# Retention and soft mixture of experts on one core: tiles of 128 positions of one batch in place of 64 positions of two

## The chip, the cores and the metric

The kernel runs on one core of a Trainium2 chip. The time is device microseconds for one execution, the median of several runs. One more execution was recorded by the hardware profiler; all rows of the profile come from it. The engines are called as in the profile: PE (TensorE, matmuls; PEld its weight loads), DVE (VectorE), ACT (ScalarE), POOL (GpSimd), SP (SyncE, which issues most transfers).

## The reference

```python
# q, k, v: 8 batches x 8 heads x 576 positions x 64, float32
scores = q @ k^T / sqrt(64)
gamma  = 1 - 2 ** (-5 - head)
ret    = scores * where(i >= j, gamma ** (i - j), 0)
x      = (ret @ v), heads side by side: 4608 tokens x 512
# soft mixture of experts, 8 experts of 4 slots, hidden size 1024
logits = x @ phi                                  # 4608 x 32
d      = softmax(logits over the 4608 tokens)
slot_input = d^T @ x                              # 32 x 512
slot_out   = relu(slot_input[e] @ w1[e]) @ w2[e]  # per expert
c      = softmax(logits over the 32 slots)
out    = c @ slot_out
```

The decay factors into a factor of the key's position and one of the query's, so a chunk of positions needs the masked scores inside the chunk and, for all earlier chunks, one 64 x 64 state per head, which is the sum of k^T v so far.

## The kernel before, in words

The program has two parts. A loop over `NT` = 36 tiles computes the retention, the transposed output, the logits and the running sums of the softmax over tokens. Behind the loop come the experts' two layers and the output product.

A tile before holds 64 positions of two batches: rows 0 to 63 of the 128 partitions are one batch, rows 64 to 127 the other. There are 9 chunks of 64 for each of the four pairs of batches. Eight heads stand as four pairs `a` with `j` = 0, 1. Each step of a tile is a method:

- `stage_k(t)`: four PE transposes of k (L151), copied to `kt` by ACT (L152). It is done for the tile ahead.
- `scale(t)`: POOL multiplies v by its decay (L136) and builds `gb`, the query's decay for this chunk (L138). Also one tile ahead.
- `stage_a(t)`: scores, 16 products of 64 x 64 (L160), masked into `s` by one DVE operation (L163).
- `stage_c(t)`: adds k^T v to the state in PSUM (L194, 16 products), and ACT copies the state to `sb` (L197).
- `stage_i(t, same)`: queries times the state so far (L177), in two pieces of 8 products, the second behind a small DVE copy `seen` (L181) that reads what the first wrote.
- `stage_b(t)`: adds v^T s to the same PSUM tile `px` (L207, 16 products); DVE multiplies by `gb` into the output tile `x` (L214).
- `stage_d(t)`: transposes x back to rows (L221, ACT L223).
- Group work, one part per tile and one group per four tiles: `group_1` the logits (L235) and running maximum, `group_e` the exponentials, `group_2` a transpose (L273), `group_3` the product with x (L282) added to `acc` (L288), `softmax_c` the softmax over slots (L294 to L308).

Products with 64 rows and 64 columns use one quarter of the PE array each, at a position given by the rows of their operands and of their output.

The order of all engines is written out by hand: each engine does its instructions in the order of the source. For a tile it is a, c, first i, k of the next tile, group parts and d, second i, b. SP issues the loads in that order too: `tok` holds k, v and the transposed q of each tile; k and v go to one of four slots `kv` (K behind c, V behind b, four tiles ahead), q to one of three slots `qs`, and the experts' weights, 41 units of 512 KB, to `ws`, spread over the loop.

PSUM has eight banks: two for `ps_n` (k, d, logits, group product), two for the state, two for scores (with a corner `pse` for small transposes), two for `px`.

Of the kernel before, what the change touches and what calls it, by code (L numbers as in the profile page):

```python
# [20 lines left out]
C = 64  # L21
NC = S // C
NT = B // 2 * NC
# [4 lines left out]
NR = 7  # L28
CST = ((0, C), (C, NC * H), (C + NC * H, NC * NP), (C + NC * (H + NP), NP * C))
NCST = C + NC * (H + NP) + NP * C  # L30
# [4 lines left out]

@with_exitstack
def retention_softmoe(ctx, tc, tok, phi, wun, cst, msel, out):
    nc = tc.nc
    PS = bass.MemoryType.PSUM
# [11 lines left out]
    ps_st = ctx.enter_context(tc.tile_pool(name="ps_st", bufs=1, space=PS))  # L51
    tiles_only = ExitStack()
# [6 lines left out]
    s = slots.tile([P, 2, NP, C], F32, name="sT")  # L59
# [3 lines left out]
    tri, vt, cf, g0 = (cs_[:, o:o + n] for o, n in CST)  # L63
    vt = vt.rearrange("p (n h) -> p n h", n=NC)
    cf = cf.rearrange("p (n a) -> p n a", n=NC)
    g0 = g0.rearrange("p (a i) -> p a i", a=NP)
    gb = [cpool.tile([P, NP, C], F32, name=f"gb{i}") for i in range(2)]
    phs = cpool.tile([P, NP, NS], F32, name="phs")
    ms = cpool.tile([P, 2 * P], F32, name="ms")
    ident = cpool.tile([P, P], F32, name="ident")  # L70
    sb = [cpool.tile([P, 2, NP, D], F32, name=f"sb{i}") for i in range(2)]
# [26 lines left out]
    nc.scalar.dma_start(out=cs_, in_=cst)  # L98
    K, V = slice(0, 512), slice(512, 1024)
# [7 lines left out]
    late = [(phs, phi), (ms, msel)]  # L107
# [8 lines left out]
    pss = ps_s.tile([P, 2, 512], F32, name="pss")  # L116
    pse = pss[:, 0, NP * C:NP * C + P]
# [15 lines left out]

    def scale(t):
        v = vn(t)
        nc.gpsimd.tensor_tensor(  # L136
            out=v, in0=v, in1=vt[:, t % NC, :].unsqueeze(2).broadcast_to([P, H, D]), op=ALU.mult)
        nc.gpsimd.tensor_tensor(  # L138
            out=gb[t % 2], in0=g0, in1=cf[:, t % NC, :].unsqueeze(2).broadcast_to([P, NP, C]), op=ALU.mult)

    def bank_n():
        return ps_n.tile([P, NP, P], F32, name="pn")

    def mtile():
        return bank_n().rearrange("p a i -> p (a i)")
# [8 lines left out]
    def stage_a(t):  # L154
        q = qT(t)
        ps = pss[:, :, 0:NP * C].rearrange("p j (a i) -> p j a i", a=NP)
        for a in range(NP):
            for j in range(2):
                for r in range(2):
                    nc.tensor.matmul(ps[half(r), j, a, :], lhsT=kt[half(j), a, half(r)],  # L160
                                     rhs=q[half(j), a, half(r)], start=True, stop=True,
                                     skip_group_check=True)
        nc.vector.tensor_tensor(out=s, in0=ps, in1=tri.unsqueeze(1).unsqueeze(2).broadcast_to([P, 2, NP, C]),  # L163
                                op=ALU.mult)

    def stage_i(t, same):
        if not same:
            PX[t] = ps_x.tile([P, 2, 512], F32, name="px")[:, :, 0:NP * C].rearrange(
                "p r (c i) -> p r c i", c=NP)
        if t % NC == 0:  # L170
            return
        px = PX[t]
        for z in range(2):
            for al in range(2):
                for j in range(2):
                    r, a = (j if same else 1 - j), 2 * z + al
                    nc.tensor.matmul(px[half(al), r, 2 * j + z, :], lhsT=sb[t % 2][half(j), r, a, :],  # L177
                                     rhs=qT(t)[half(j), a, half(r)], start=(not same and z == 0),
                                     stop=False, skip_group_check=True)
        if not same:  # L180
            nc.vector.tensor_copy(out=sm("seen")[D:P], in_=px[D:P, 0, NP - 1, 0:1])  # L181

    def stage_c(t):
        n = t % NC
        if n == NC - 1:
            return
        if n == 0:
            ST[0] = ps_st.tile([P, 2, 512], F32, name="pst")[:, :, 0:NP * D].rearrange(
                "p r (a d) -> p r a d", a=NP)
        k, v = kn(t), vn(t)  # L190
        for a in range(NP):
            for r in range(2):
                for j in range(2):
                    nc.tensor.matmul(ST[0][half(j), r, a, :], lhsT=k[half(r), 2 * a + j, :],  # L194
                                     rhs=v[half(r), 2 * a + j, :], start=(n == 0 and a == 0),
                                     stop=(n == NC - 2), skip_group_check=True)
        nc.scalar.copy(out=sb[(t + 1) % 2], in_=ST[0])  # L197

    def stage_b(t):
        v = vn(t)  # L200
        px = PX.pop(t)
        for z in range(2):
            for j in range(2):
                for al in range(2):
                    for r in range(2):
                        a = 2 * z + al
                        nc.tensor.matmul(px[half(al), r, 2 * j + z, :], lhsT=v[half(r), 2 * a + j, :],  # L207
                                         rhs=s[half(r), j, a, :], start=(t % NC == 0 and z == 0 and j == 0),
                                         stop=True, skip_group_check=True)
        x = ring.tile([P, NP, P], F32, name="x")  # L210
        xv = x.rearrange("p c (r i) -> p r c i", r=2)
        for c in ((slice(0, 2), slice(2, 4)) if t == NT - 1 else (slice(0, 4),)):
            n = c.stop - c.start
            nc.vector.tensor_tensor(out=xv[:, :, c], in0=px[:, :, c],  # L214
                                    in1=gb[t % 2][:, c].unsqueeze(1).broadcast_to([P, 2, n, C]), op=ALU.mult)
        xT[t] = x
# [54 lines left out]
    def group_2(g):  # L271
        et, alpha = gstate[g]
        nc.tensor.transpose(pse, et, ident)  # L273
        en = gpool.tile([P, P], F32, name="en")
        nc.scalar.copy(out=en, in_=pse)
        gstate[g] = (en, alpha)
# [14 lines left out]
    def softmax_c(g, pn=None):  # L291
        if pn is None:
            pn = pse
            nc.tensor.transpose(pn, ltg[g], ident)  # L294
# [16 lines left out]
    delta = ms[:, 0:P]  # L311
    negmask = ms[:, P:2 * P]

    scale(0)
    stage_k(0)
    for t in range(NT):
        g, r = divmod(t - 4, 4)
        group = t >= 4
        stage_a(t)
        stage_c(t)  # L320
        stage_i(t, False)
        load_kv(t + NKV, K)
        while issued[0] < min(NW, NW * (t + 1) // (NT - 3)):
            load_w(ws[issued[0]])
# [11 lines left out]
        if group and r == 2:  # L336
            stage_d(4 * g + 3)
        if t == NT - 2:
            group_3(g)
        if group and r == 3:  # L340
            if t < NT - 1:
                group_3(g)
                softmax_c(g)
            else:
                stage_d(NT - 4, True)
                mo = mrun[(NG - 2) % 2]
                nc.tensor.transpose(pse, mo.broadcast_to([P, P]), ident)
                mm = gpool.tile([P, 4, NS], F32, name="et")
                mom = mm[:, 0, :]
                nc.vector.tensor_reduce(out=mom, in_=pse.rearrange("p (i s) -> p s i", i=4),  # L350
                                        axis=AX.X, op=ALU.max)
# [9 lines left out]
    stb = ps_st.tile([P, 2, 512], F32, name="pst")  # L361
    wb, pm = stb[:, 0], stb[:, 1]
    pl = logits(pm, NG - 1, 0, 3)
    hm = [slots.tile([P, 1024], F32, name="kv3").rearrange("p (c e s) -> p c e s", c=4, e=NE)]
    sim = [slots.tile([P, 2, NE, NS], F32, name=x) for x in ("qs0", "sT")]
    nc.gpsimd.memset(sim[0], 0.0)
    nc.gpsimd.memset(sim[1], 0.0)
# [62 lines left out]
    for i in range(4):  # L430
        nc.tensor.matmul(pr[i * NS:(i + 1) * NS, 0:1], lhsT=en[:, i * NS:(i + 1) * NS],
                         rhs=tri[:, C - 1:C], start=True, stop=True, skip_group_check=True)
# [40 lines left out]
    identr = cpool.tile([P, 2, P], F32R, name="gb0")[:, 0]  # L473
    nc.gpsimd.tensor_copy(out=identr, in_=ident)
    cs = []
    ctw = [cpool.tile([P, NP, P], F32R, name=n) for n in ("sb0", "sb1")]
# [43 lines left out]
    p1 = [wb, mtile()]  # L520
# [136 lines left out]
def unpack(o):  # L657
    o = o.reshape(2, NG, 2, C, 4, 256).transpose(1, 4, 2, 3, 0, 5)
    o = o.reshape(B // 2, NC, 2, C, DM).transpose(0, 2, 1, 3, 4)
    return o.reshape(B * S, DM)  # L660
# [55 lines left out]
```

## Time and profile before

| what | value |
|---|---|
| median of 3 runs | 259.07 us (258.59 to 259.28) |
| the profiled execution | 260.98 us |
| its span, first to last instruction | 259.2 us |
| PE busy | 206.6 us (80%), 5571 matmuls and 5571 weight loads |
| DVE, ACT, POOL busy | 101.0, 90.5, 62.1 us |
| moved by DMA | 72.52 MB, 280 GB/s on the mean |
| mean granted PE clock | 0.950 |

How to read it: the profile lists one record for each matmul and one for each weight load, and an fp32 product makes two of each (an fp32 transpose one). A record's length is its latency; products on different parts of the array overlap, so the distance between starts tells what a product costs. "issue" is time in which an engine waited for nothing that the profile shows. The queue "q8 instruction" carries the engines' programs.

### The profile page before, as it was taken

How to read it: one execution, taken by the hardware profiler on the slowest of the kernel's cores; microseconds unless marked ns; L12 is line 12 of the kernel's file. 1: busy time of each engine (PE TensorE's matmuls, PEld its weight loads, DVE VectorE, ACT ScalarE, POOL GpSimd, SP SyncE). 2: the span in 40 equal slices, each digit the busy share in tenths (PEclk: the TensorE clock that was granted, in tenths of full speed). 3: DMA queues.
4: the chain of work that ended last, by engine and by line, in shares of the span. 5: the costliest groups of instructions: out<-in, count | busy, mean ns of one | idle time of the engine just before them, and what ended most of it. 6: DMA issues, size and time to landing. Idle time of an engine off the chain costs nothing.

```text
span 259.2 us, 12312 instructions
## 1 busy us (share of the span) xinstructions
PE 206.6 (80%) x5571; PEld 152.9 (59%) x5571; DVE 101.0 (39%) x250; ACT 90.5 (35%) x198; POOL 62.1 (24%) x83
## 2 busy tenths in 40 slices
PE   7759698788759886977887879887997799999830
PEld 6648485575648565666565567566673235666620
DVE  0324043543524534352354354352354423155740
ACT  2312243343333353245143335334221033243730
POOL 1824043242223234033223423322120010000000
PEclk9998799999998999799999999998999999999985
DMA  6998788988796989788876998884220999976895
GB/s 199 389 388 276 282 265 279 325 290 293 236 325 190 304 310 304 227 303 286 287 265 226 320 317 303 292 310 147 85 83 3 326 414 409 408 293 262 338 402 235
DMA packets 27556, 72.52 MB, mean 280 GB/s; under 512 B 3056, under 2 KB 3440, under 8 KB 27504
## 3 DMA queue, kind: packets, MB, share of 16 engines
q1 hardware_dynamic: 27360, 71.51, 78.2%
q8 instruction: 44, 0.72, 1.1%
q10 hardware_dynamic: 144, 0.22, 0.2%
q14 instruction: 8, 0.07, 0.1%
HBM read 62.28 MB, written 9.44 MB: 277 GB/s over the span
## 4 chain that ended last, share of the span: by engine, by line
PE 66%; issue 12%; DVE 9%; ACT 6%; DMA 2%; POOL 0%; DVEq 0%; SPq 0%; ACTq 0%; POOLq 0%
PE px L177 9%; PE pn L151 8%; PE pn L221 6%; PE pst L574 6%; PE px L207 5%; PE pst L194 5%; PE pss L160 5%; PE pn L282 4%; DVE x L214 4%; PE pn L235 3%; PE po L599 3%; PE pst L526 3%; PE pn L526 3%; ACT kt L152 2%; DMA kv<-in_tok 2%
## 5 line engine op out<-in xcount | busy, mean ns | idle before, releaser
L138 POOL TENSOR_TENSOR gb<-cst 128x256 f32<-128x256 f32 x36 | 22.1, 615 | 117.0 <-DVE x L214 117.0
L177 PE MATMUL px<-qs,sb 64*64 64x64 f32 x1024 | 32.6, 236 | 17.4 <-issue 8.9
L214 DVE TENSOR_TENSOR x<-px,gb 128x512 f32<-128x512 f32 (+1 forms) x37 | 24.9, 676 | 50.1 <-PE px L207 49.8
L136 POOL TENSOR_TENSOR kv<-kv,cst 128x512 f32<-128x512 f32 x36 | 37.6, 1044 | 7.4 <-DMA kv<-in_tok 7.4
L177 PEld LDWEIGHTS px<-qs,sb 64*64 64x64 f32 x1024 | 23.6, 140 | 26.5 <-issue 14.4
L197 ACT COPY sb<-pst 128x512 f32<-128x512 f32 x32 | 18.8, 587 | 57.4 <-PE pst L194 57.4
L152 ACT COPY kt<-pn 128x512 f32<-128x512 f32 x36 | 21.1, 586 | 35.1 <-PE pn L151 34.9
L160 PE MATMUL pss<-qs,kt 64*64 64x64 f32 x1152 | 27.1, 225 | 6.3 <-issue 5.4
L207 PE MATMUL px<-sT,kv 64*64 64x64 f32 x1152 | 26.6, 228 | 2.9 <-issue 2.9
L163 DVE TENSOR_TENSOR sT<-pss,cst 128x512 f32<-128x512 f32 x36 | 24.6, 684 | 10.4 <-PE pss L160 8.9
L194 PE MATMUL pst<-kv 64*64 64x64 f32 x1024 | 24.0, 224 | 5.4 <-issue 5.1
L160 PEld LDWEIGHTS pss<-qs,kt 64*64 64x64 f32 x1152 | 22.8, 139 | 8.2 <-issue 6.9
L151 PE MATMUL pn<-ident,kv 128*128 128x128 f32 x144 | 24.2, 290 | 2.7 <-issue 2.7
L207 PEld LDWEIGHTS px<-sT,kv 64*64 64x64 f32 x1152 | 22.8, 144 | 4.0 <-issue 3.9
L194 PEld LDWEIGHTS pst<-kv 64*64 64x64 f32 x1024 | 20.5, 138 | 6.2 <-issue 5.8
L221 PE MATMUL pn<-ident,x 128*128 128x128 f32 x132 | 22.8, 299 | 1.1 <-issue 0.4
L223 ACT COPY x<-pn 128x512 f32<-128x512 f32 x33 | 19.4, 588 | 8.8 <-PE pn L221 8.3
L221 PEld LDWEIGHTS pn<-ident,x 128*128 128x128 f32 x132 | 16.0, 149 | 4.8 <-ACT kt L152 3.7
L151 PEld LDWEIGHTS pn<-ident,kv 128*128 128x128 f32 x144 | 15.4, 143 | 2.5 <-DMA kv<-in_tok 0.2
L561 DVE COPY ws<-po 128x512 f32<-128x512 f32 x15 | 10.1, 690 | 8.4 <-PE po L599 8.3
L559 ACT COPY ws<-po 128x512 f32<-128x512 f32 x15 | 8.7, 589 | 10.5 <-PE po L599 10.4
L282 PE MATMUL pn<-x,en 128*32 128x512 f32 x64 | 10.7, 649 | 1.1 <-ACT kt L152 0.6
(143 smaller groups left out, 203.1 us busy)
## 6 DMA issues: line engine op xcount, KB each, us to landing
ws<-in_w SPq DMA_DIRECT2D x61, 512.0 KB, 6.0
kv<-in_tok SPq DMA_DIRECT2D x66, 256.0 KB, 4.2
qs<-in_tok SPq DMA_DIRECT2D x36, 256.0 KB, 4.2
out<-ws SPq DMA_DIRECT2D x14, 512.0 KB, 3.9
kv<-in_tok SPq DMA_DIRECT2D x3, 512.0 KB, 7.0
kv<-in_w SPq DMA_DIRECT2D x3, 512.0 KB, 5.0
out<-kv SPq DMA_DIRECT2D x3, 512.0 KB, 6.2
out<-ws SPq DMA_DIRECT2D x2, 256.0 KB, 3.2
```

The source lines that it names most:

```text
L136: nc.gpsimd.tensor_tensor(out=v, in0=v, in1=vt[:, t % NC, :].unsqueeze(2).broadcast_to([P, H, D]), op=ALU.mult)
L138: nc.gpsimd.tensor_tensor(out=gb[t % 2], in0=g0, in1=cf[:, t % NC, :].unsqueeze(2).broadcast_to([P, NP, C]), op=ALU.mult)
L151: nc.tensor.transpose(pk[:, a, :], k[:, 2 * a:2 * a + 2, :].rearrange("p j d -> p (j d)"), ident)
L152: nc.scalar.copy(out=kt, in_=pk)
L160: nc.tensor.matmul(ps[half(r), j, a, :], lhsT=kt[half(j), a, half(r)], rhs=q[half(j), a, half(r)], start=True, stop=True, skip_group_check ...
L163: nc.vector.tensor_tensor(out=s, in0=ps, in1=tri.unsqueeze(1).unsqueeze(2).broadcast_to([P, 2, NP, C]), op=ALU.mult)
L177: nc.tensor.matmul(px[half(al), r, 2 * j + z, :], lhsT=sb[t % 2][half(j), r, a, :], rhs=qT(t)[half(j), a, half(r)], start=(not same and z ...
L194: nc.tensor.matmul(ST[0][half(j), r, a, :], lhsT=k[half(r), 2 * a + j, :], rhs=v[half(r), 2 * a + j, :], start=(n == 0 and a == 0), stop=( ...
L207: nc.tensor.matmul(px[half(al), r, 2 * j + z, :], lhsT=v[half(r), 2 * a + j, :], rhs=s[half(r), j, a, :], start=(t % NC == 0 and z == 0 an ...
L214: nc.vector.tensor_tensor(out=xv[:, :, c], in0=px[:, :, c], in1=gb[t % 2][:, c].unsqueeze(1).broadcast_to([P, 2, n, C]), op=ALU.mult)
L221: nc.tensor.transpose(pn[:, a, :], xT[t][:, a, :], ident)
L282: nc.tensor.matmul(pp[i * NS:(i + 1) * NS, :], lhsT=en[:, i * NS:(i + 1) * NS], rhs=xN[4 * g + i].rearrange("p a i -> p (a i)"), start=Tru ...
```

## The change

A tile now holds 128 positions of one batch. A batch has four chunks of 128 positions and 64 left over; the left-over halves of two batches share a ninth tile (chunk number `NCH` = 4), so there are again 36 tiles. Tiles of the two batches of a pair take turns (`tile_order`).

- Scores: 16 products again. A 128 x 128 block of scores is cut in four 64 x 64 squares, of which the upper one is zero and is never computed. So half of the products stream 128 query columns and half 64. `s` is twice as wide, its zero square is written once ahead of the loop. The order of k and v rows is swapped by halves for four of the heads.
- The mask takes three DVE operations: two of 64 rows x 256, one of 128 x 512.
- `stage_i` is one piece of 8 products with 128 columns streaming; the `seen` copy is gone. It uses one state per batch (`sb[b % 2]`), in the ninth tile both.
- `stage_c` has 8 products over all 128 rows, 64 columns wide; the state copy is half as large.
- `stage_b` has 8 products over all 128 rows of v, with 128 columns streaming.
- `gb` is twice as wide and built once for the two batches of a pair.
- The order becomes a, d (remainders 1 and 2), k, group parts, i, group parts, c, b. `group_3` moves from remainder 3 to remainder 2, between i and c. K and V are loaded together behind b. A PSUM bank of its own (`ps_m`) takes logits, group product and small transposes.
- Constants: the table `g0` is 128 wide and has a transfer of its own; `ms` is loaded late, into a free q slot; the `x` ring has 6 slots in place of 7.

Counted in PE instructions (matmuls and weight loads), a tile with group work on the mean has 196 in place of 292.

```diff
-C = 64
-NC = S // C
-NT = B // 2 * NC
+NCH = 4
+NT = 36
-NR = 7
+NR = 6
+def tile_order():
+    order = []
+    for b0 in range(0, B, 2):
+        for c in range(NCH):
+            order.append((b0, c))
+            order.append((b0 + 1, c))
+        order.append((b0, NCH))
+    return order
...
+    ps_m = ctx.enter_context(tc.tile_pool(name="ps_m", bufs=1, space=PS))
-    s = slots.tile([P, 2, NP, C], F32, name="sT")
+    s = slots.tile([P, 2, NP, P], F32, name="sT")
...
     nc.scalar.dma_start(out=cs_, in_=cst)
+    nc.scalar.dma_start(out=g0, in_=gtab)
-    late = [(phs, phi), (ms, msel)]
+    late = [(phs, phi)]
...
     def scale(t):
-        v = vn(t)
+        v, c = vn(t), order[t][1]
         nc.gpsimd.tensor_tensor(
-            out=v, in0=v, in1=vt[:, t % NC, :].unsqueeze(2).broadcast_to([P, H, D]), op=ALU.mult)
-        nc.gpsimd.tensor_tensor(
-            out=gb[t % 2], in0=g0, in1=cf[:, t % NC, :].unsqueeze(2).broadcast_to([P, NP, C]), op=ALU.mult)
+            out=v, in0=v, in1=vt[:, c, :].unsqueeze(2).broadcast_to([P, H, D]), op=ALU.mult)
+        if t and order[t - 1][1] == c:
+            gi[t] = gi[t - 1]
+            return
+        gi[t] = 1 - gi[t - 1] if t else 0
+        o = gb[gi[t]]
+        if c < NCH:
+            nc.gpsimd.tensor_tensor(out=o, in0=g0, in1=cf[:, c, :].unsqueeze(2).broadcast_to([P, NP, P]),
+                                    op=ALU.mult)
+            return
...
     def stage_a(t):
+        for al in range(2):
+            for z in range(2):
+                a = 2 * z + al
+                for h in range(2):
+                    r = slice((h ^ z) * D, (h ^ z) * D + D)
+                    cols = slice(h * 64, (h + 1) * 64 if c == NCH else P)
+                    for j in range(2):
+                        e = slice(j * D, (j + 1) * D)
+                        nc.tensor.matmul(ps[r, j, a, cols], lhsT=kt[e, a, r], rhs=q[e, a, cols],
+                                         start=True, stop=True, skip_group_check=True)
+        for z in range(2):
+            r, aa = slice(z * D, (z + 1) * D), slice(2 * z, 2 * z + 2)
+            nc.vector.tensor_tensor(out=s[r, :, aa, 0:64], in0=ps[r, :, aa, 0:64],
+                                    in1=tri[r].unsqueeze(1).unsqueeze(2).broadcast_to([D, 2, 2, 64]), op=ALU.mult)
+        if c < NCH:
+            nc.vector.tensor_tensor(out=s[:, :, :, 64:P], in0=ps[:, :, :, 64:P],
+                                    in1=gm.unsqueeze(1).broadcast_to([P, 2, NP, 64]), op=ALU.mult)
+            return
...
+    def stage_i(t):
+        for i in range(2 if c == NCH else min(c, 1)):
+            cols = slice(i * 64, (i + 1) * 64) if c == NCH else slice(0, P)
+            for a in range(NP):
+                for j in range(2):
+                    r = slice(a % 2 * D, (a % 2 + 1) * D)
+                    e = slice(j * D, (j + 1) * D)
+                    nc.tensor.matmul(px[r, j, a // 2, cols], lhsT=sb[i if c == NCH else b % 2][e, a, :],
+                                     rhs=qT(t)[e, a, cols], start=(i == 0 and a < 2), stop=False,
+                                     skip_group_check=True)
+    def stage_b(t):
+        for j in range(2):
+            for z in range(2):
+                for al in range(2):
+                    a = 2 * z + al
+                    nc.tensor.matmul(px[al * D:(al + 1) * D, j, z, :], lhsT=v[:, 2 * a + j, :],
+                                     rhs=s[:, j, a, :], start=(c == 0 and z == 0), stop=True,
+                                     skip_group_check=True)
...
+    def stage_c(t):
         for a in range(NP):
             for j in range(2):
+                nc.tensor.matmul(pst[j * D:(j + 1) * D, a, :], lhsT=k[:, 2 * a + j, :],
+                                 rhs=v[:, 2 * a + j, :], start=(c == 0 and a == 0 and b % 2 == 0),
+                                 stop=(c == NCH - 1), skip_group_check=True)
+        nc.scalar.copy(out=sb[b % 2], in_=pst)
...
         stage_a(t)
-        stage_c(t)
-        stage_i(t, False)
-        load_kv(t + NKV, K)
-        while issued[0] < min(NW, NW * (t + 1) // (NT - 3)):
-            load_w(ws[issued[0]])
+        if group and r == 1:
+            stage_d(4 * g + 1)
+        if group and r == 2:
+            stage_d(4 * g + 3)
         if t + 1 < NT:
             stage_k(t + 1)
             scale(t + 1)
         if group and r == 0:
             group_1(g)
             stage_d(4 * g)
-            group_e(g)
         if group and r == 1:
-            stage_d(4 * g + 1)
             group_2(g)
-            stage_d(4 * g + 2)
...
-        stage_i(t, True)
+        stage_i(t)
         load_q(t + NQ)
-        stage_b(t)
-        load_kv(t + NKV, V)
+        if t == NT - NQ:
+            ms = slots.tile([P, 2 * P], F32, name=f"qs{t % NQ}")
+            nc.sync.dma_start(out=ms, in_=msel)
+        while issued[0] < min(NW, NW * (t + 1) // (NT - 3)):
+            load_w(ws[issued[0]])
...
+        if group and r == 0:
+            group_e(g)
+        if group and r == 1:
+            stage_d(4 * g + 2)
+        if group and r == 2:
+            group_3(g)
+        stage_c(t)
+        stage_b(t)
+        load_kv(t + NKV)
```

More of the change, by code (lines that the diff above doesn't have):

```diff
@@ L154, in stage_a @@
     def stage_a(t):
+        c = order[t][1]
         q = qT(t)
-        ps = pss[:, :, 0:NP * C].rearrange("p j (a i) -> p j a i", a=NP)
+        ps = ps_s.tile([P, 2, 512], F32, name="pss").rearrange("p j (a i) -> p j a i", a=NP)
+        for al in range(2):
+            for z in range(2):
+                a = 2 * z + al
+                for h in range(2):
+                    r = slice((h ^ z) * D, (h ^ z) * D + D)
[4 more added lines that the diff above has]
+                                         start=True, stop=True, skip_group_check=True)
@@ new lines, in stage_a @@
+        for z in range(2):
+            r, aa = slice((1 - z) * D, (2 - z) * D), slice(2 * z, 2 * z + 2)
+            nc.vector.tensor_tensor(out=s[r, :, aa, 64:P], in0=ps[r, :, aa, 64:P],
+                                    in1=tri[r].unsqueeze(1).unsqueeze(2).broadcast_to([D, 2, 2, 64]), op=ALU.mult)
+            nc.vector.memset(s[z * D:(z + 1) * D, :, aa, 64:P], 0.0)
+    def stage_i(t):
+        b, c = order[t]
+        px = ps_x.tile([P, 2, 512], F32, name="px").rearrange("p j (z i) -> p j z i", z=4)
+        PX[t] = px
+        for i in range(2 if c == NCH else min(c, 1)):
[7 more added lines that the diff above has]
+                                     skip_group_check=True)
@@ new lines, in stage_b @@
+    def stage_b(t):
+        b, c = order[t]
+        v = vn(t)
+        px = PX.pop(t)
+        for j in range(2):
+            for z in range(2):
+                for al in range(2):
[3 more added lines that the diff above has]
+                                     skip_group_check=True)
+        x = ring.tile([P, NP, P], F32, name="x")
+        xv = x.rearrange("p (j z) i -> p j z i", j=2)
+        g = gb[gi[t]].rearrange("p (j z) i -> p j z i", j=2)
+        for j in ((0, 1) if t == NT - 1 else (slice(0, 2),)):
+            nc.vector.tensor_tensor(out=xv[:, j], in0=px[:, j, 0:2], in1=g[:, j], op=ALU.mult)
+        xT[t] = x
@@ L157, in stage_a @@
+    def stage_c(t):
+        b, c = order[t]
+        if c == NCH:
+            return
+        if c == 0 and b % 2 == 0:
+            ST[0] = ps_st.tile([P, 2, NP, D], F32, name="pst")
+        pst = ST[0][:, b % 2]
+        k = kn(t)
+        v = vn(t)
         for a in range(NP):
             for j in range(2):
[L159 to L197, printed above, removed]
@@ L272, in group_2 @@
         et, alpha = gstate[g]
-        nc.tensor.transpose(pse, et, ident)
+        pe = mtile()
+        nc.tensor.transpose(pe[:, 0:P], et, ident)
         en = gpool.tile([P, P], F32, name="en")
-        nc.scalar.copy(out=en, in_=pse)
+        nc.scalar.copy(out=en, in_=pe[:, 0:P])
         gstate[g] = (en, alpha)
@@ L292, in softmax_c @@
         if pn is None:
-            pn = pse
-            nc.tensor.transpose(pn, ltg[g], ident)
+            pn = mtile()
+            nc.tensor.transpose(pn[:, 0:P], ltg[g], ident)
         ln = pn[:, 0:P].rearrange("p (i s) -> p i s", i=4)
@@ L472, in retention_softmoe @@
     ct = {}
[L473 removed]
+    identr = cpool.tile([P, NP, P], F32R, name="gb0")[:, 0]
     nc.gpsimd.tensor_copy(out=identr, in_=ident)
     cs = []
[L476 removed]
+    ctw = [cpool.tile([P, NP, P], F32R, name=n) for n in ("gb1", "g0", "acc")]
     h1 = [slots.tile([P, 512], F32, name=f"qs{i + 1}") for i in range(2)]
```

129 lines of the change are left out of this document (66 added, 63 removed).

## The prediction

> **What bounds the kernel now.** The page and a table by stretches come first: how much of the span the tile loop takes, and how busy TensorE (PE) is in it. (Columns of the table: stretch, length, busy time and instructions of PE, weight loads, DVE, ACT and POOL, granted clock, DMA share, GB/s.)
>
> ```profile
> span 259.2 us, 12312 instructions
> PE 206.6 (80%) x5571; PEld 152.9 (59%) x5571; DVE 101.0 (39%) x250; ACT 90.5 (35%) x198; POOL 62.1 (24%) x83
> ...
> q8 instruction: 44, 0.72, 1.1%
> ```
>
> ```profile
> 6.87:190.67 183.80, 147.55 (x4948) 117.50 (x4939) 73.68 (x185) 67.46 (x146) 58.26 (x73) 0.95 0.82 277
> 190.67:259.20 68.53, 53.87 (x594) 30.53 (x587) 27.16 (x64) 21.13 (x50) 2.61 (x4) 0.94 0.75 293
> ```
>
> The loop over 36 tiles runs from the first matmul of L160 (6.87 us) to the last of L207 (190.67): 183.8 us, 5.1 us a tile. No other engine passes 74 us there; DMA is 82% busy. So the order on PE sets the time, and the question is what PE waits for. The chain of waits in that stretch, and two stretches of four tiles with the same work:
>
> ```profile
> by line: issue 16.1%; PE px L177 12.5%; PE pn L151 11.3%; PE pn L221 8.8%; PE px L207 7.4%; PE pst L194 7.2%; PE pss L160 7.0%; PE pn L282 5.7%; DVE x L214 4.9%; PE pn L235 4.9%; ACT kt L152 2.6%; DVE acc L288 2.0%; ACT et L243 1.3%; ACT en
> ```
>
> ```profile
> 119.90:142.00 22.10, 17.12 (x570) 12.94 (x562) 8.78 (x25) 8.18 (x18) 6.47 (x8) 1.00 0.77 259
> 142.00:161.10 19.10, 15.71 (x551) 12.55 (x555) 8.64 (x24) 7.60 (x17) 6.56 (x9) 1.00 0.92 317
> ```
>
> The largest item is no engine: "issue", 16.1% of 183.8 = 29.6 us in which PE stood still and waited for nothing recorded. Equal work took 22.1 or 19.1 us. The timeline shows what such a hole looks like:
>
> ```profile
> 100.89 0.65 PE L160 MATMUL pss<-qs,kt 64*64 64x64 f32 x32
> ...
> 101.35 0.29 PE L194 MATMUL pst<-kv 64*64 64x64 f32 x7
> ...
> 103.59 0.85 PE L194 MATMUL pst<-kv 64*64 64x64 f32 x25 [1.95 <-issue]
> ```
>
> It is in the middle of 32 equal passes whose operands are all there. The next fence counts the instructions between two holes (table by stretches: 60.96 to 64.72), and the DMA queues over the second hole:
>
> ```profile
> 60.96:64.72 3.76, 3.75 (x127) 2.56 (x128) 1.57 (x4) 1.17 (x2) 1.17 (x2) 1.00 0.82 284
> ```
>
> ```profile
> q8 instruction: 1, 0.02, 2.4%
> ...
> 66.16 0.35 PE L207 MATMUL px<-sT,kv 64*64 64x64 f32 x9 [1.24 <-issue]
> ```
>
> 127 matmuls and 128 weight loads: 255 instructions, then a hole, with one instruction packet of 0.02 MB in it. The page agrees: 11142 PE instructions in 44 instruction packets are 253 each. I read the holes as **waits for PE's own code**: a block of about 256 instructions was used up in 3.76 us and the next one was there 5.2 us after the last (60.96 to 66.16). By the Trainium skill ("Runtime: NRT & Kernel Launch", Instruction fetch mechanics) code comes in 16 KiB blocks of 256 instructions, and crossing a boundary is "mostly hidden"; the block size agrees with this trace, the hiding does not.
>
> **Prices on PE.** One clean tile:
>
> ```profile
> 152.98 1.08 PE L235 MATMUL pn<-x,phs 128*32 128x128 f32 x32
> 153.99 0.66 PE L221 MATMUL pn<-ident,x 128*128 128x128 f32 x4
> 154.58 0.46 PE L177 MATMUL px<-qs,sb 64*64 64x64 f32 x16
> 154.86 0.65 PE L207 MATMUL px<-sT,kv 64*64 64x64 f32 x32
> 155.32 0.65 PE L160 MATMUL pss<-qs,kt 64*64 64x64 f32 x32
> 155.79 0.65 PE L194 MATMUL pst<-kv 64*64 64x64 f32 x32
> 156.90 0.29 PE L177 MATMUL px<-qs,sb 64*64 64x64 f32 x4 [0.46 <-DVE x L214]
> ```
>
> By starts, 32 passes on 64x64 squares take 0.46 us (154.86 to 155.32): eight rounds of 0.058, four squares at once. L235 works on 128 rows by 32 columns, 128 columns streaming: 32 passes, four at once, are eight rounds R and a switch W to the next shape, 1.01 us; L221's four transposes are 4R + W = 0.59. So R = 0.105 and W = 0.17 us. All times below are from these three.
>
> **The change, part by part (per tile, PE).** An fp32 product is two passes.
> - Scores (stage_a): still 16 products, but half stream 128 columns in place of 64. Each square gets 4 passes of 128 and 4 of 64: 4 x 0.105 + 4 x 0.058 = 0.65, was 0.46. No row mixes widths on the squares: if the two column halves took turns it would be 1.3; all three kinds of row above run squares side by side, so I take 0.65.
> - State into queries (stage_i): 16 passes of 128 columns on four squares, 0.42, was 2 x 16 passes of 64, 0.46. It is one piece now; the `seen` copy and its round trip go.
> - State update (stage_c): 16 passes, 128 rows by 64 columns, 64 streaming. Two column tiles at once: 8 x 0.058 = 0.46, as before. Stage_b: 16 passes with 128 streaming: 8 x 0.105 = 0.84, was 0.46. The shape is not in the trace. Bounds: no overlap (twice that, 0.92 and 1.68), or four at once as L235 (half). Two tiles fill the columns, so I take two at once.
> - Shape switches: a, then k, then i, then c and b, then a are 4 a tile; before there were 2 (c/i to k, k to i/b). Two more: 0.34 us, 12 us over 36 tiles. The Trainium skill ("TensorEngine Tiling (Array Packing)", Key Properties) says that a change of tiling mode drains TensorE, which speaks against the change; the trace agrees, with W for its price.
>
> So PE has **more** to do: per tile 0.19 - 0.04 + 0.38 + 0.34 = +0.87 us. Without holes the change loses.
>
> Now other engines:
>
> ```profile
> L163 DVE TENSOR_TENSOR sT<-pss,cst 128x512 f32<-128x512 f32 x36 | 24.6, 684 | 10.4 <-PE pss L160 8.9 <-PE pst L194 1.2
> L214 DVE TENSOR_TENSOR x<-px,gb 128x512 f32<-128x512 f32 x35 | 24.2, 690 | 49.4 <-PE px L207 49.1
> L585 DVE TENSOR_TENSOR kt<-pn,kt 64x256 fp32r<-64x256 f32 x2 | 0.9, 428 | 1.0 <-ACT kt L584 1.0
> L181 DVE COPY seen<-px 64x1 f32<-64x1 f32 x32 | 5.2, 163 | 9.2 <-PE px L177 8.4
> L136 POOL TENSOR_TENSOR kv<-kv,cst 128x512 f32<-128x512 f32 x36 | 37.6, 1044 | 7.4 <-DMA kv<-in_tok 7.4
> L138 POOL TENSOR_TENSOR gb<-cst 128x256 f32<-128x256 f32 x36 | 22.1, 615 | 117.0 <-DVE x L214 117.0
> ```
>
> ```profile
> 143.80 0.65 PE L207 MATMUL px<-sT,kv 64*64 64x64 f32 x32
> 144.26 0.65 PE L160 MATMUL pss<-qs,kt 64*64 64x64 f32 x32
> ...
> 144.58 0.69 DVE L214 TENSOR_TENSOR x<-px,gb 128x512 f32<-128x512 f32 x1 [1.74 <-PE px L207]
> ```
>
> ```profile
> PEld px L177 <- DVE x L214: 10.3, 13, 1.1
> ```
>
> - Masking s: one DVE operation of 684 ns becomes two of 64x256 (nearest row: 428 ns) and one of 684: 1.54 us. Hidden while PE does k, i and c behind stage_a (0.59 + 0.59 + 0.63 = 1.81 against 0.3 to start, 144.26 to 144.58, and 1.6). Behind a waiting b stands all of the next tile. DVE's total goes from 74 to about 74 + 36 x 0.86 - 5 = 100 us of some 160.
> - i's wait for x (10.3 us today) goes: a and k, 1.4 us, now stand between b and i, against 0.3 + 0.69. Where softmax_c's small operations delay x, the next logits wait instead; I take 0.3 us in one tile of four.
> - POOL: gb is 128x512 (as L136, 1.04 us) but made 20 times, not 36; ACT's state copy halves. Both hidden: POOL has 58 us of work in 184.
> - Loads: K is no longer fetched before V, the pair goes in one transfer behind b. SP's queue now holds q, weights, kv; the slots still give three tiles (14 us) of lead. ms moves into a free q slot near the end. At nothing; were kv late, k and all behind it would wait.
> - Start: constants grow.
>
> ```profile
> cst<-in_cst ACTq DMA_DIRECT2D x1, 214.0 KB, 3.8
> ...
> 6.90:20.20 13.30, 8.89 (x359) 7.52 (x353) 3.69 (x7) 3.52 (x6) 6.95 (x9) 0.94 1.01 380
> ```
>
>  195 + 256 KB instead of 214, at 380 GB/s: +0.6 us ahead of the first tile.
>
> **The sum.** Tiles repeat in fours (group work by t mod 4). With a 0.82, k or d 0.59 (0.42 behind another transpose), logits or group product 1.01, i 0.59, c 0.63, b 0.84: remainder 0: a, k, logits, d, i, c, b = 5.07, + 0.3 wait; 1: a, d, k, a transpose 0.11, i, d, c, b = 4.59; 2: a, d, k, i, group product, c, b = 4.90; 3: a, k, 0.11, i, c, b = 3.58, and DVE's ring (a, 0.3, s 1.6, b) the same. 18.4 us for four. Eight fours and four first tiles of 3.6: 162. First chunks have no i and last ones no c: some 3.5 us off where PE sets the time. 159 us against 183.8: -25.
>
> Holes left: 196 instructions in 4.6 us are 256 in 6.0, above the 5.2 a block took; the densest 256 (a remainder-3 tile, then a, k and some logits) take 5.2. I leave 2 us. So -25 + 2 + 0.6 = -22. The profiled execution took 260.98 us (span 259.2, the rest around it): 239; it stands 1.9 above the median of 259.07, so **237 us**. The tail, 68.5 us, is taken as it is.
>
> **Rivals.**
> 1. *The holes come back through DMA.* The loop's bytes in 160 us are 277 x 184/160 = 318 GB/s, and the clean stretch already showed 317 at 92% busy. If a block then took one of today's holes longer (5.2 + 1.3 = 6.5 us), the loop's 26 blocks (6700 instructions) would each miss about 0.5: +14, 251 us. Against: that same stretch had few holes.
> 2. *Column tiles do not overlap with 128 rows (slower).* b and c take 1.68 and 0.92: 36 x 0.84 + 32 x 0.46 = +45, of which 3 hide in waits for s: 279 us. It decides from +0.6 us a tile on. Against: L235.
> 3. *The widths in stage_a take turns*: +0.65 x 36 = +23, less 3: 257 us.
> 4. *The holes are not code.* They would stay, 29.6 us: 266 us, slower. For: code is fetched as regularly where there is no hole. Against: the 255 instructions between two of them. The "mostly hidden" of the Trainium skill quoted above would mean this case.
> 5. *Better than summed*: switches overlap with waits and no hole is left: 231 us.
>
> **How the numbers follow.** Forecast (230 to 243 by itself) 0.66; rival 1 0.12; 2 0.06; 3 0.06; 4 0.05; 5 0.05. The range 229 to 252 takes in the forecast, 1 and 5. About 0.3% is what can be told from no change; faster: 0.66 + 0.12 + 0.05 and most of 3 = 0.88, slower 0.10, same 0.02.
>
> **What would show it.** "issue" in the chain of the loop under 6 us; 0.84 us from the start of b to the next a less one switch; 16 passes of c in 0.46; 32 of a in 0.65; about 31 instruction packets in place of 44 (7900 instructions); PE's busy time per tile up, not down. b at 1.7 us, or holes as before, would prove it wrong.

## The result, and the profile after

The changed kernel takes 235.36 us (median of 4 runs, 232.57 to 235.86) where the kernel before takes 259.17 us (4 runs, 258.59 to 261.53). The ratio is 0.9044, 95% interval 0.8952 to 0.9135. The forecast was 237 us. Ratios, here and below, go by the fast runs alone and are not quotients of the medians, which take in all runs.

The page of the changed kernel, its head, its engines and the queue that carries programs:

```profile
span 233.2 us, 9102 instructions
...
PE 216.9 (93%) x3971; PEld 159.9 (69%) x3971; DVE 131.8 (56%) x302; ACT 82.4 (35%) x198; POOL 62.5 (27%) x72
...
q8 instruction: 31, 0.51, 0.9%
```

The table by stretches, loop and tail (columns as in the prediction):

```profile
6.80:168.82 162.02, 158.18 (x3360) 124.51 (x3360) 104.46 (x237) 59.49 (x146) 58.02 (x60) 1.00 0.88 314
168.82:233.20 64.38, 53.62 (x589) 30.58 (x587) 27.14 (x64) 21.03 (x50) 3.04 (x4) 0.96 0.79 311
```

The chain of waits in the loop:

```profile
by line: PE px L229 20.6%; PE pss L190 18.7%; PE pn L258 11.8%; PE pst L250 10.6%; PE px L217 10.0%; PE pn L175 9.6%; PE pm L320 5.7%; PE pm L272 5.4%; DVE sT L195 2.6%; DVE sT L198 1.7%; issue 1.2%; PE pm L311 0.5%; DVE sT L203 0.5%; ACT x
```

PE's waits of the changed kernel (what PE waited for: us in all, times, longest):

```profile
PE px L229 <- DVE sT L198: 1.9, 4, 0.6
...
PE px L229 <- DVE sT L205: 0.7, 2, 0.5
```

The loop went from 183.80 to 162.02 us. "issue" was the largest item of its chain, 29.6 us; it is now 1.2% of 162.02 = 1.9 us. PE is busy 98% of the loop, and for longer than before (158.18 against 147.55 us): it does more and stands still less. The profiled execution took 234.99 us against 260.98, 26.0 less: 21.8 from the loop, 4.1 from the tail (68.53 to 64.38), 0.1 from the start.

**Where the holes lie.** The next table counts PE's instructions of the kernel before, each time from the start of one hole to the start of a later one:

```profile
25.57:40.54 14.97, 12.12 (x382) 10.10 (x381) 3.78 (x10) 5.91 (x13) 3.94 (x5) 0.89 0.79 269
73.25:101.64 28.39, 23.28 (x760) 19.07 (x760) 10.83 (x28) 11.19 (x24) 9.27 (x12) 0.94 0.83 276
```

763 and 1520 are three and six times 256 less 5 and 16; those few are semaphore instructions of PE's queue, which the table does not count. Counted with them, all 13 stretches of over 1 us in this loop in which neither a matmul nor a weight load ran start at the same place of a block of 256 instructions. At these block ends PE stood still for 24.0 us in all ("issue" is 29.6), in the changed loop for 0.7 (of 1.9). The records of the queue "q8 instruction" say when a block's packet had landed: in the loop before, 30 of 38 blocks started 1.2 to 1.6 us after their packet; in the changed loop 6 of 26; in none of the loops of this document did a block start sooner than 1.2 us after it.

**The clock.** The granted clock is 0.95 in the loop before and 1.00 in the changed one. In the loop before, five stretches of 3.4 us had half the clock, at 18.48, 28.72, 76.51, 103.81 and 178.91 us; the second of them:

```profile
28.72:32.13 3.41, 3.41 (x72) 2.70 (x64) 0.44 (x2) 1.61 (x5) 0.00 (x0) 0.50 0.67 270
```

Each begins within 1.1 us of the end of a hole, and the four longest holes (2.55, 2.68, 2.20 and 1.95 us) have one each. Five times 3.4 us at half clock cost at most 8.5 us, an estimate that takes PE as the bound in all of them. So a long hole seems to cost more than the time in which PE stands still; no run tried the clock by itself.

One tile without a hole, with the group product (timeline of PE; the last two rows begin the next tile):

```profile
140.49 1.05 PE L229 MATMUL px<-sT,kv 128*64 128x128 f32 x16
141.47 0.90 PE L190 MATMUL pss<-qs,kt 64*64 64x128 f32 x32
142.30 0.66 PE L258 MATMUL pn<-ident,x 128*128 128x128 f32 x4
...
143.32 0.67 PE L217 MATMUL px<-qs,sb 64*64 64x128 f32 x16
143.92 1.06 PE L320 MATMUL pm<-x,en 128*32 128x512 f32 x8
144.92 0.69 PE L250 MATMUL pst<-kv 128*64 128x64 f32 x16
145.43 1.04 PE L229 MATMUL px<-sT,kv 128*64 128x128 f32 x16
146.41 0.90 PE L190 MATMUL pss<-qs,kt 64*64 64x128 f32 x32
```

By starts, 16 passes of stage_c take 0.51 us (144.92 to 145.43), the 16 of stage_b with the switch behind them 0.98 (145.43 to 146.41), the 32 of stage_a with a switch 0.83 (141.47 to 142.30), and stage_i with its switch 0.60 (143.32 to 143.92). The whole tile, b to b, is 4.94.

### The profile page after: what moved, and what is told of

It reads as the page before. It is cut to its first block, busy times and chain, and to the rows that moved or that the text cites. A ratio compares the mean times of both kernels' runs of the same rounds, so it can differ in the third digit from the quotient of the medians.

```text
span 233.2 us, 9102 instructions
## 1 busy us (share of the span) xinstructions
PE 216.9 (93%) x3971; PEld 159.9 (69%) x3971; DVE 131.8 (56%) x302; ACT 82.4 (35%) x198; POOL 62.5 (27%) x72
## 4 chain that ended last, share of the span: by engine, by line
PE 87%; DVE 4%; ACT 2%; issue 2%; DMA 1%; DVEq 0%
PE px L229 14%; PE pss L190 13%; PE pn L258 8%; PE pst L250 7%; PE px L217 7%; PE pn L175 7%; PE pm L614 6%; PE pm L272 4%; PE pm L320 4%; PE po L639 3%; PE pst L566 3%; PE pn L566 3%; PE px L126 2%; DVE sT L195 2%; DVE sT L198 1%
## 5 line engine op out<-in xcount | busy, mean ns | idle before, releaser
L229 PE MATMUL px<-sT,kv 128*64 128x128 f32 x576 | 38.6, 275 | 2.7 <-DVE sT L198 1.9
L195 DVE TENSOR_TENSOR sT<-pss,cst 64x256 f32<-64x256 f32 x72 | 30.3, 421 | 11.9 <-PE pss L190 9.4
L190 PE MATMUL pss<-qs,kt 64*64 64x64 f32 (+1 forms) x1152 | 32.9, 248 | 1.4 <-ACT kt L176 0.7
L229 PEld LDWEIGHTS px<-sT,kv 128*64 128x64 f32 x576 | 30.9, 137 | 4.7 <-PE pst L250 2.4
L250 PEld LDWEIGHTS pst<-kv 128*64 128x64 f32 x512 | 17.5, 137 | 10.1 <-issue 8.1
L250 PE MATMUL pst<-kv 128*64 128x64 f32 x512 | 21.9, 228 | 0.0
L158 POOL TENSOR_TENSOR gb<-g,cst 128x512 f32<-128x512 f32 x16 | 16.7, 1041 | 12.0 <-DVE x L236 12.0
L217 PE MATMUL px<-qs,sb 64*64 64x128 f32 (+1 forms) x512 | 18.8, 267 | 0.0
L253 ACT COPY sb<-pst 128x256 f32<-128x256 f32 x32 | 11.7, 367 | 13.0 <-PE pst L250 12.6
L217 PEld LDWEIGHTS px<-qs,sb 64*64 64x64 f32 x512 | 12.4, 132 | 4.7 <-DVE sT L195 3.4
```

Of the source, the lines that this page charges most:

```text
L190: nc.tensor.matmul(ps[r, j, a, cols], lhsT=kt[e, a, r], rhs=q[e, a, cols], start=True, stop=True, skip_group_check=True)
L195: nc.vector.tensor_tensor(out=s[r, :, aa, 0:64], in0=ps[r, :, aa, 0:64], in1=tri[r].unsqueeze(1).unsqueeze(2).broadcast_to([D, 2, 2, 64]), ...
L217: nc.tensor.matmul(px[r, j, a // 2, cols], lhsT=sb[i if c == NCH else b % 2][e, a, :], rhs=qT(t)[e, a, cols], start=(i == 0 and a < 2), st ...
L229: nc.tensor.matmul(px[al * D:(al + 1) * D, j, z, :], lhsT=v[:, 2 * a + j, :], rhs=s[:, j, a, :], start=(c == 0 and z == 0), stop=True, ski ...
L250: nc.tensor.matmul(pst[j * D:(j + 1) * D, a, :], lhsT=k[:, 2 * a + j, :], rhs=v[:, 2 * a + j, :], start=(c == 0 and a == 0 and b % 2 == 0) ...
```

## Experiments

**All wide products cut in two.** Every product of stages a, i and b that streams 128 columns becomes two of 64. The computation, its layout, DVE's work and the loads stay; a tile again has 292 PE instructions.

```diff
-                for h in range(2):
+                for h, hh in ((0, 0), (1, 1)) if c == NCH else ((0, 0), (1, 1), (0, 1)):
...
-                    cols = slice(h * 64, (h + 1) * 64 if c == NCH else P)
+                    cols = slice(hh * 64, (hh + 1) * 64)
...
-                for al in range(2):
-                    a = 2 * z + al
-                    nc.tensor.matmul(px[al * D:(al + 1) * D, j, z, :], lhsT=v[:, 2 * a + j, :],
-                                     rhs=s[:, j, a, :], start=(c == 0 and z == 0), stop=True,
+                for hh, al in ((0, 0), (0, 1), (1, 0), (1, 1)):
+                    a, cols = 2 * z + al, slice(hh * 64, (hh + 1) * 64)
+                    nc.tensor.matmul(px[al * D:(al + 1) * D, j, z, cols], lhsT=v[:, 2 * a + j, :],
+                                     rhs=s[:, j, a, cols], start=(c == 0 and z == 0 and hh == 0), stop=True,
```

> The changed kernel, but every product that streams 128 columns is cut into two of 64: a tile has 292 PE instructions again, streams the same columns and computes the same. Theory (the holes are waits for PE's code): streaming grows only by the rounds, 12 x 0.058 for 0.65 in scores, 8 x 0.058 for 0.42 in states, 16 x 0.058 for 0.84 in stage_b, +0.18 us a tile or 6.5 us; the holes come back, 25 to 40 us of issue in the loop, 255 to 268 us in all. Rival (the holes belonged to the old layout of two batches, or to the transfers): 235 + 6.5 = 242 us, issue below 4 us.

Measured: 260.98 us (256.44 to 262.99, 10 runs) against 261.61 for the kernel before (13 runs), ratio 0.9939 (0.9837 to 1.0041). The whole gain is gone. Its loop by stretches, PE's waits, and the program queue:

```profile
6.95:191.75 184.80, 166.53 (x4835) 138.32 (x4838) 104.86 (x237) 59.59 (x146) 57.90 (x60) 0.99 0.81 276
```

```profile
PE px L229 <- issue: 6.5, 6, 1.9
PE pss L190 <- issue: 3.2, 3, 1.5
PE px L217 <- issue: 2.6, 5, 0.7
PE pn L258 <- issue: 1.7, 1, 1.7
```

```profile
q8 instruction: 43, 0.70, 1.1%
```

The holes are back, in front of stages that had none. The chain of this loop has "issue" at 8.6% (15.9 us), less than the 25 to 40 expected. Of the 22.8 us that the loop is longer than the changed kernel's, 14.0 are holes and 8.3 more busy time of PE (166.53 against 158.18). At block ends PE stands still for 16.0 us here.

**Only stage_b cut**, the same edit as above for that stage alone: 228 instructions a tile.

> The changed kernel with only stage_b cut into 64 columns: 228 PE instructions a tile. Theory: +0.09 us a tile of streaming, 3.2 us, and 228 instructions at 5.2 us per 256 are 4.6 us, about what a tile takes: a few holes, 3 to 8 us, 240 to 246 us. Rival (no code limit): 238.5 us.

Measured: 245.63 us (244.99 to 246.93), ratio 0.9430 (0.9358 to 0.9502). Its loop, and the largest of PE's waits:

```profile
7.22:180.04 172.82, 162.15 (x3939) 131.69 (x3942) 104.42 (x237) 59.65 (x146) 57.54 (x60) 0.99 0.85 294
```

```profile
PE pss L190 <- issue: 5.0, 5, 3.1
PE px L229 <- issue: 3.5, 3, 1.9
```

The chain has 5.6% of this loop, 9.7 us, in "issue", more than the 3 to 8 us expected; the time is in the range. So with 196, 228 and 292 instructions a tile, the same layout and the same loads, the holes are 1.9, 9.7 and 15.9 us (0.7, 9.0 and 16.0 at block ends), and the instruction packets 31, 36 and 43.

**The layout before, with fewer instructions.** Two products of 64 columns become one of 128 in stages a, i and c, which gives 196 instructions a tile too. What is computed changes: half of the heads use another head's operand in these three stages, so only its time is of use.

```diff
-        for a in range(NP):
+        for a in (0, 2):
...
-                    nc.tensor.matmul(ps[half(r), j, a, :], lhsT=kt[half(j), a, half(r)],
-                                     rhs=q[half(j), a, half(r)], start=True, stop=True,
+                    nc.tensor.matmul(ps[half(r), j, a:a + 2, :], lhsT=kt[half(j), a, half(r)],
+                                     rhs=q[half(j), a, :], start=True, stop=True,
```

> The kernel before with its layout, DVE, ACT, POOL work and transfers unchanged, but scores, states and state update each issue 8 products of 128 columns in place of 16 of 64 (leaves out: half of the heads get the product of another head's operand, so the output is not the reference's). A tile has 196 PE instructions and streams as much as before. Theory: the holes go (issue under 6 us in the loop) and the time falls to 228 to 236 us, as far as the changed kernel, with none of its layout. Rival (the gain came from the layout): 255 to 259 us.

Measured: 232.61 us (230.60 to 235.09), ratio 0.8899 (0.8791 to 0.9006). Its loop, and PE's waits:

```profile
7.05:162.47 155.42, 136.00 (x3363) 101.17 (x3366) 73.27 (x185) 67.36 (x146) 58.42 (x73) 1.00 0.92 326
```

```profile
PE px L176 <- DVE x L213: 8.5, 13, 1.3
PE pss L160 <- issue: 5.4, 7, 1.4
```

None of the new stages of 128 rows by 64 columns is in this kernel, and it gains about as much: "issue" fell from 29.6 to 11.7 us (7.5% of 155.42; under 6 had been expected), and PE's busy time from 147.55 to 136.00, of which up to 8.5 us can be the clock (0.95 before, 1.00 here). Fewer and wider products are enough for a gain of this size. The new layout adds 22 us of PE's busy time to the loop (158.18 against 136.00) for the same count; what it gives back is the wait of i for x (8.5 us here) and 9.8 of the 11.7 us of "issue". Of these 11.7, 7.1 us stand at block ends: this denser loop uses up its code sooner, 256 instructions in 5.9 us against 6.2.

**More DMA, first try.** One more transfer of 256 KB a tile, always into the same free weight slot.

```diff
+        if issued[0] < NW - 3:
+            nc.sync.dma_start(out=ws[NW - 1][:, 0:512], in_=tok[t, :, 1024:1536])
```

> The changed kernel with one more transfer of 256 KB per tile into a weight slot that is not yet in use: 314 GB/s in the loop become about 370. Theory (PE sets the time, DMA has some room left): within +4 us, issue under 5 us. Rival (fuller queues delay the code blocks and the holes return): +8 to +14 us with 8 us or more of issue.

Measured: 243.18 us (242.73 to 243.70), ratio 0.9336 (0.9264 to 0.9408). The waits of SP's queue and of PE:

```profile
SPq L382 <- DMA ws<-in_tok: 74.6, 30, 4.3
```

```profile
PE pn L175 <- DMA kv<-in_tok: 9.1, 12, 1.5
```

"issue" stays at 0.8% of the loop. The extra transfers write one slot, so each waited in SP's queue for the one before, and the load of k behind them was late. The holes of the rival did not come, but the time is a price of the edit's order and does not decide between the two theories.

**More DMA, without the wait:** the same transfers, 28 of them in place of 31, taking turns over six slots.

```diff
+        if issued[0] < NW - 7:
+            nc.sync.dma_start(out=ws[NW - 1 - t % 6][:, 0:512], in_=tok[t, :, 1024:1536])
```

> As the run with one more transfer of 256 KB per tile, but the extra transfers go round six weight slots, so that none waits for the one before and SP's queue is not held up. Theory (PE sets the time, DMA has room up to some 390 GB/s): within +3 us of the changed kernel, no holes. Rival (DMA near its bound): +6 us or more, k and v late as in that run.

Measured: 237.13 us (235.20 to 238.81), ratio 0.9172 (0.9057 to 0.9286). Its loop by stretches:

```profile
6.40:168.77 162.37, 157.41 (x3362) 124.35 (x3363) 106.10 (x237) 59.43 (x146) 58.17 (x60) 1.00 0.96 360
```

The loop takes 162.37 us in place of 162.02 while DMA moves 360 GB/s in place of 314, and "issue" is 1.1% of it. A DMA share of 0.96 brings no holes. The profiled execution is the fastest of the four, and the median is 1.8 us above the changed kernel's, so a small price is not ruled out.

**The price of a shape switch.** A tiny product is put between stage_k and stage_i. In the control it has stage_i's shape; in the other kernel its shape is 128 rows by 32 columns, which neither neighbour has, so there is one more switch in each tile.

```diff
 # control
+        nc.tensor.matmul(px[0:D, 0, 2, 0:1], lhsT=ident[0:D, 0:D], rhs=ident[0:D, 0:1], start=True, stop=True,
+                         skip_group_check=True)
 # one more switch
+        nc.tensor.matmul(px[0:NS, 0, 2, 0:1], lhsT=ident[:, 0:NS], rhs=ident[:, 0:1], start=True, stop=True,
+                         skip_group_check=True)
```

> The changed kernel with one product of 64 rows, 64 columns and one streaming column ahead of stage_i in every tile, on the square shape that stage_i has itself (its output is read by nobody). The control for the next run. Two passes more, no shape switch except in the 8 tiles without stage_i: +1 to +4 us on 235. If products of any size cost a full round and a wait, +5 us or more.

> The same small product, but of 128 rows by 32 columns, between the transposes (128 by 128) and stage_i (64 by 64): one shape switch more in every tile. Theory (W = 0.17 us on PE's path in each switch): 36 x 0.17 = 6 us above the run with the square shape. Rival (switches hide behind the waits that are there anyway): within 1 us of it.

Measured: 235.75 us (234.66 to 236.46), ratio 0.9093 (0.9012 to 0.9175), and 237.18 us (236.68 to 237.69), ratio 0.9152 (0.9075 to 0.9229). The control stands 0.4 us above the changed kernel, where 1 to 4 were expected. The medians of the two are 1.4 us apart where 6 were forecast; the intervals overlap, so the timeline decides. One tile with the group product in the control, and in the kernel with the added switch:

```profile
140.54 1.04 PE L231 MATMUL px<-sT,kv 128*64 128x128 f32 x16
...
145.58 1.05 PE L231 MATMUL px<-sT,kv 128*64 128x128 f32 x16
```

```profile
141.02 1.05 PE L231 MATMUL px<-sT,kv 128*64 128x128 f32 x16
...
143.32 0.60 PE L175 MATMUL pn<-ident,kv 128*128 128x128 f32 x4
143.85 0.22 PE L211 MATMUL px<-ident 128*32 128x1 f32 x2
144.00 0.67 PE L219 MATMUL px<-qs,sb 64*64 64x128 f32 x16
...
146.11 1.04 PE L231 MATMUL px<-sT,kv 128*64 128x128 f32 x16
```

From b to b that is 5.04 us in the control and 5.09 with the added switch (4.94 in the changed kernel): the added switch costs 0.05 us, with its product 0.15. In the undisturbed tiles of the other three remainders it is 0.05 or 0.06 too (4.74 and 4.79, 3.71 and 3.77, 5.21 and 5.26). That is not the W = 0.17 of the prediction. Behind a product with one column streaming, almost nothing is in flight when the shape changes, while W was read behind full stages; that this makes the difference is my reading, and no run varies it.

**The kernel before, with the expert layer's first sum in a PSUM tile of its own.** This takes up the part of the tail that nobody had forecast.

```diff
-    p1 = [wb, mtile()]
+    p1 = [pbank(), mtile()]
```

> The kernel before with one edit behind the loop: the first expert layer's first sum is written to a PSUM bank of its own instead of the other half of the two-bank tile that the small transposes use. Theory (the tail became 4.1 us shorter since these two stand in separate tiles after the change, so the products no longer wait for VectorE's reading of the transposes): the stretch from the first expert product to the first of the second layer, 17.5 us before, falls to about 15.3, and the time by 2 us. Rival (the tail's gain lies in where code blocks fall): 17.5 us, no change.

Measured: 259.62 us (255.67 to 262.39, 12 runs), ratio 0.9919 (0.9848 to 0.9990). Four fences, three of them tables by stretches: the first expert layer in this kernel; the tail of the kernel before in three stretches; PE's wait in the expert layer before, from its list of waits; and the tail of the changed kernel.

```profile
198.29:213.87 15.58, 15.58 (x138) 4.96 (x141) 5.14 (x19) 3.00 (x10) 0.95 (x1) 1.00 0.78 299
```

```profile
190.67:198.02 7.35, 6.20 (x85) 4.54 (x78) 4.30 (x15) 2.25 (x7) 1.66 (x3) 1.00 0.03 9
198.02:215.50 17.48, 15.86 (x138) 4.94 (x142) 5.24 (x19) 3.01 (x10) 0.95 (x1) 1.00 0.81 313
215.50:259.20 43.70, 31.81 (x376) 21.05 (x368) 17.62 (x30) 15.87 (x33) 0.00 (x0) 0.90 0.84 332
```

```profile
PE pst L526 <- DVE et L299: 1.6, 2, 0.9
```

```profile
168.82:175.43 6.61, 6.22 (x81) 4.56 (x79) 4.39 (x15) 2.15 (x7) 2.08 (x3) 1.00 0.00 0
175.43:191.00 15.57, 15.57 (x137) 4.95 (x141) 5.14 (x19) 3.01 (x10) 0.95 (x1) 1.00 0.76 285
191.00:233.20 42.20, 31.83 (x376) 21.06 (x368) 17.61 (x30) 15.86 (x33) 0.00 (x0) 0.93 0.93 369
```

In the kernel before, PE's first layer (L526) wrote the same PSUM tile `pst` from which DVE still read logits for `softmax_c` (L299), and waited 1.6 us. With a tile of its own the layer takes 15.58 us, as in the changed kernel (15.57), whose bank `ps_m` parts the two in another way. That is 1.9 of the tail's 4.1 us.

**k transposed ahead (a try for a better kernel).** Since DMA had room in the run above, k's transpose of each tile is packed beside q and loaded; stage_k's four PE transposes and ACT's copy go. Packing it moves part of the work out of the kernel into the layout of its input.

```diff
-            nc.sync.dma_start(out=qs[t % NQ], in_=tok[t, :, 1024:1536])
+            nc.sync.dma_start(out=qs[t % NQ], in_=tok[t, :, 1024:2048])
...
-            stage_k(t + 1)
```

> The changed kernel, but k's transpose of every tile is packed beside q by the host and comes by DMA (512 KB in one transfer in place of 256 KB); the four transposes of k and ACT's copy of them are gone (192 matrix instructions a tile), and one weight slot fewer is loaded ahead. Theory (PE's own work sets the loop, and DMA has room): 0.42 us and a shape switch leave PE in remainders 0 to 2 of t, while DVE's ring of some 3.6 us keeps remainder 3 where it is; 27 tiles by 0.3 to 0.45 is 8 to 12 us, so 223 to 228 us where the changed kernel takes 235. Rival (the transfers bound the loop once 9.4 MB more have to be moved): the loop cannot get under some 56 MB / 360 GB/s = 155 us and the weights come later, so 230 to 238 us, and PE waits for kv or the mask copies.

Measured: 237.19 us (235.54 to 238.36), ratio 0.9084 (0.9014 to 0.9153): no gain over the changed kernel. Its loop by stretches, the chain of waits in that loop, and what DMA moved in 40 slices of the span:

```profile
5.86:169.46 163.60, 147.86 (x3223) 112.90 (x3226) 106.03 (x237) 40.51 (x111) 58.18 (x60) 0.99 0.97 369
```

```profile
by line: DMA kv<-in_tok 18.9%; PE px L222 14.8%; PE pss L183 11.5%; PE pn L251 9.0%; PE pst L243 6.7%; PE px L210 6.6%; DVE sT L188 5.3%; PE pm L265 4.9%; PE pm L313 4.5%; issue 3.7%; DVE sT L191 3.4%; POOL kv L149 3.2%; DVE x L229 2.8%; PO
```

```profile
GB/s 187 415 407 401 407 395 410 373 339 412 396 328 367 402 357 411 402 364 297 379 388 385 399 409 403 338 273 353 108 3 76 402 411 403 411 408 330 357 407 310
```

The rival was right. PE's busy time fell by 10.3 us (158.18 to 147.86) and the loop did not get shorter: the loads of k and v now lead the chain (18.9% of 163.60 = 31 us), and many slices of the loop stand at 395 to 415 GB/s. The room for more bytes ends there, in this order of transfers. "issue" is 3.7% of this loop, 6.1 us, of which 2.9 stand at block ends.

## Why the prediction was right, point by point

- **Holes are waits for PE's code: shown.** The holes stand at the ends of blocks of 256 instructions, and a block that PE waited for starts 1.2 to 1.6 us after its packet has landed. Cutting products in two, in the same layout, brings the holes back in steps (1.9, 9.7, 15.9 us), and joining products in the old layout takes most of them away. About 31 instruction packets were forecast, and 31 counted. Rival 4 (the holes are no code, 266 us) falls. The sentence of the Trainium skill that was quoted with it ("Runtime: NRT & Kernel Launch", Instruction fetch mechanics: "mostly hidden") holds for the changed kernel, not for the one before: what decides is how long PE takes over each 256 instructions.
- **Holes left.** Forecast 2 us from the densest 256 instructions, measured 1.9. Only 0.7 of these stand at block ends, so the size is in part luck.
- **Prices.** Stage_c: forecast 0.46, seen 0.51 up to the next stage. Stage_b: 0.84 and a switch W, seen 0.98 together; stage_a: 0.65 + 0.17 against 0.83. So two column tiles do run side by side over 128 rows, and mixed widths do not take turns: rivals 2 (279 us) and 3 (257 us) fall.
- **Tile periods.** Forecast 5.37, 4.59, 4.90 and 3.58 for remainders 0 to 3, 18.4 for four. The tiles without a disturbance, b to b, took 5.21, 4.64, 4.94 and 3.62 (the third is the tile shown above): 18.41. Each is within 0.16 us, and the errors cancel.
- **The loop.** Forecast 159 + 2 = 161, measured 162.02.
- **DVE's delay** was at another place than forecast. The 0.3 us in one tile of four were meant for the logits behind softmax_c's small operations; no such wait is in PE's list. PE waited for the mask copies instead, 1.9 + 0.7 us ahead of stage_b (L229). The size was nearly the same (nine times 0.3 is 2.7), the mechanism was not. The prediction's own numbers left the mask 0.1 us short (1.81 us of cover for 0.3 + 1.6), which it called hidden.
- **Rival 1 (the holes come back through DMA, 251 us): refuted** at the rate that it named and above it, by the run with 360 GB/s. (Its sum, 26 blocks by 0.5 us, is 13 and not 14.) At 369 GB/s, in the last run, some holes do come back (2.9 us at block ends).
- **The clock has no term in the prediction.** All prices were read where the clock was 1.00, and the sum holds for a loop at 1.00, which the changed loop is. That the 183.8 us before hold up to 8.5 us of half clock was overlooked; the loop's 159 us were built up from prices, so the forecast did not suffer.
- **The start.** Forecast +0.6 us for larger constants; the loop begins at 6.80 in place of 6.87. The term was sized as if its bytes delayed the first tile, and they did not.
- **The tail was the term that was mis-sized.** "Taken as it is" was its step; it became 4.1 us shorter. 1.9 of these are the PSUM tile above: the change text says that `ps_m` takes logits and small transposes, and this reaches the tail's `softmax_c`, which the prediction did not follow beyond the loop. 0.7 lie in the first stretch (7.35 to 6.61): in the chain before, an exponential's two steps on DVE and ACT (L415 and L417, 0.30 and 0.32 us) stand between PE's instructions there, and in the chain after they do not. This is read from the chains and was not tried by itself. The last 1.5 us lie behind PE's last product: from its end to the end of the span it is 10.6 us before and 9.1 after, while PE's work in the last stretch takes 33.1 us in both. Two kernels with the layout and the tail of before took 9.1 (the one with joined products) and 11.1 us (the one with the PSUM tile) there, and those with the changed tail 9.1 to 10.0, so I put the 1.5 down to scatter of the last stores; what scatters them stays open.

- **The sum.** Against the profiled execution 239 was forecast and 234.99 measured, 4.0 less: the tail -4.1, the start -0.7, the loop +1.0 (the rest is rounding). The step from there to the median took 1.9 off, as the profiled execution before stands that much above its median; the changed kernel's stands 0.4 below its own. These 2.3 us hid, by luck, more than half of the tail's error, so 237 is nearer to 235.36 than its terms are.
- **Rival 5 (better than summed, 231 us)** was not it either: the tiles took what was summed, and some holes are left.

## What to carry to other kernels

Divide PE's instructions by 256 and ask what time PE spends on each block; where that is below what a block of code takes to come (a packet landed every 4.7 us on the mean in the loop before), a kernel gets faster by issuing fewer, wider instructions, even when the array does more. Look at the densest blocks too: the loop with joined products takes 5.9 us for 256 on the mean and still waits. Count a new layout's work by starts of neighbouring rows, not by lengths of records, and take the price of a switch from a place that is as full as the one where it will stand. When a buffer is given a home of its own, look for every later stage that shared the old one: here a change made for the loop paid again in the tail.

## What the runs showed of the hardware that was not expected

- **Two loops with 292 instructions a tile take the same time although PE's work differs.** The loop before has 9887 PE instructions in 183.80 us, that with cut products 9673 in 184.80: 4.8 and 4.9 us for each 256, with PE busy for 147.55 (half clock in it) and 166.53 us. In both, 30 blocks (of 38 and of 37) started within 1.6 us of their packet. The changed kernel has 6720 in 162.02, 6.2 us for each 256. That the supply of code sets the first two loops nearly alone is my reading of these numbers; no run changed the rate of supply.
- **Half clock behind long holes.** Beside the five stretches of the loop before, the loop with all products cut has one of 3.4 us behind its longest hole (1.9 us), and the loop with stage_b cut one behind its longest (3.1 us); the changed loop has none. The cut products were expected to add 6.5 us to PE's work and added 8.3 us to its busy time; the one stretch at half clock can be up to 1.7 of that.
- **A switch of shape behind a product of one column is nearly free**: 0.05 us in the tile shown, against the 0.17 read behind full stages. The Trainium skill ("TensorEngine Tiling (Array Packing)", Key Properties) says that a change of tiling mode drains the engine; a cost that depends on what there is to drain agrees with that.
- **More bytes cost little up to 360 GB/s.** 314 and 360 GB/s over the loop give the same loop within 0.4 us in the profiled executions; at 369 GB/s, with many slices at some 400, the loads lead the chain. Whether this is an edge or a slope, three points do not show.
- **Transfers into one slot hold the queue that issues them.** 256 KB a tile cost 0.4 us of loop over six slots (162.37 us) and 7.3 into one (169.36): SP stood 74.6 us on them, and all loads behind were late.
